# A two-layer mixer behind two attentions: the next batch's work in fewer, longer runs between the channel tiles

## The chip, the cores and the metric

The kernel runs on one core of one Trainium2 chip. The metric is device time in microseconds (us); less is better.

## The reference

For each of 8 batches there are 8 heads, 576 positions and 64 features a head. Two attentions are added, and a token mixer and a channel mixer follow:

```python
q_d = q.reshape(B, H, Sd, 4, D).mean(axis=3)          # k, v likewise; Sd = 144
out_up = np.repeat(sm_attn(q_d, k_d, v_d), 4, axis=2) # softmax attention on the pooled positions
mask = np.abs(pos[:, None] - pos[None, :]) < 4        # a band of 7 positions
out_local = softmax(where(mask, q @ k.T / 8, -1e9)) @ v
x = (out_up + out_local) as (B, 576, 512)
u = x + (relu(x.T @ w_tok1) @ w_tok2).T               # token mixer, 256 hidden
out = u + relu(u @ w_ch1) @ w_ch2                     # channel mixer, 1536 hidden
```

## The kernel before, in words

The four stages of a batch b are these (the names are those of the profile, where buffer numbers are left out).

- *Pooled attention* (`pooled`, L452 to L505, four pairs of heads): scores `sd` on TensorE (PE, L461), their maxima `mxd` and `nmd` on VectorE (L467, L468), exponentials `pd` on ScalarE (L473), transposes `td` (L480), the copy `ptd` on ScalarE (L483), the product with v `ad` (L489), and the division on VectorE (L495 to L497). A DMA then puts the result `od` beside the windows of v.
- *Local attention* (`local`, L508 to L564, five tiles of 128 or 64 positions): scores `sc` (L521), mask, maximum, difference on VectorE (L528 to L533), exponential on ScalarE (L535), sum, reciprocal and product on VectorE (L538 to L540), transposes `pT` (L544), their copy (L548), and `av` (L557), which adds both attentions in one product.
- *Token mixer* (`mix`, L582 to L671): x is split in two parts `xh` (L597, L599) so that three passes give a precise product (`mm3`, L112); `t1` (products named t by xh and W, L114), the hidden layer `hid` (L633, L635), `t2` (L621, L114), the copies `u` (L646) and their maxima `umx` (L648). Then comes the scale of the channel mixer's input, one chain for each chunk of positions (256 and 320): a maximum over the partitions by a transpose `um_t` (L573), a reduction (L576) and a broadcast `um_b` (L579); the scale by three small instructions (`pow2`, L118 to L120); and for each of the four blocks of 128 channels the split `uh` into a high half on ScalarE (L665) and a low half on VectorE (L667).
- *Channel mixer* (`first` and `second`, L722 and L747 onwards): 12 tiles of `c` by CW and uh, each of 12 products (L114), their relu split `h` in two halves (L742 on ScalarE, L744 on VectorE), then four tiles of `c` by CX and h, each of 36 products, and their addition to u (L770) and DMA out. In the text a "c product" is one of these matmuls, on 256 or 320 columns.

PSUM is divided by hand: two double banks "gg" (sd, td, sc, av, t1, t2), three banks "m" (c), one bank "g" (ad, pT, um).

The first 220 us are ordered by a planner with engine clocks (`drive`). What the change touches is the steady loop behind it, for b = 1 to 7 (L863 on). There the channel mixer of batch b is written out, and after each of its pieces `tick` issues some of batch b+1's side work: all the three stages above, and the loads of batch b+2. The side work comes from one generator (`side`, L711; `together` lets three attention pieces take turns). Each step says its engine and its estimated time; only the time of TensorE's steps is counted, and 0.05 for every step. `tick` has a target that grows with the channel mixer's columns done, up to 42 / 0.9, and issues side steps as long as their count stands below it. When a batch begins, `while ("uh", b, ch) not in made: work.go()` issues whatever is still lacking for its uh.

The loop stands outside of `tc.manual_schedule()`. So the order in which steps are issued is a priority, and the framework's scheduler still moves instructions: one that it reckons to be ready may pass one that waits. What came out is read from the built program.

Of the kernel before, what the change touches and what calls it, by code (L numbers as in the profile page):

```python
# [27 lines left out]
FR = 0.9  # L28
# [6 lines left out]
def tile_ups_attention_mixer(ctx, tc, qk, vw, vr, w1, w2, c1, c2, out):  # L35

    nc = tc.nc
    B, _, S = out.shape
# [100 lines left out]
    def may(d):  # L139
        return all(n in made for n in d[2])  # L140
# [570 lines left out]
    def side(b):  # L711

        if b < B:
            st = ready[b]
            yield from attention(st)
            m = mix(st)
            if b + 1 < B:
                m.append(ahead(b + 1))
            yield from together(m, len(m))


    def first(st, ch, places):  # L722
        b, N = st.b, CHUNKS[ch][1]
        hs = st.h[ch] = []
        for f in range(NF):
            e = yield step("P", 12 * N * 0.43e-3, ("C1", f), ("uh", b, ch),
                           *([("mixed", b)] if places[f // 3] != "h" else []), take=f"m>1{ch}")
            uh = st.uh[ch]
            ps = PM(f"c1_{b}_{ch}_{f}")[:, :N]
            for c in range(4):  # L730
                mm3(ps, lambda a: C1.fin[f][:, a, 128 * c:128 * c + 128], lambda a: uh[c][:, a], c == 0, c == 3)
            if f % 3 == 0:
                three = T([128, 3, 2, NMAX], F16, places[f // 3], f"h{b}_{ch}_{f}")
            hs.append((ps, three[:, f % 3, :, :N]))
            make(("c1", b, ch, f), e)

    def first_up(st, ch):
        b = st.b
        for f in range(NF):
            yield step("A", 0.41, ("c1", b, ch, f))  # L740
            ps, ht = st.h[ch][f]
            nc.scalar.activation(ht[:, 0], ps, AF.Relu)  # L742
            e = yield step("V", 0.46, give=f"m>1{ch}")
            nc.vector.scalar_tensor_tensor(ht[:, 1], ps, 0.0, ht[:, 0], ALU.max, ALU.subtract)  # L744
            make(("h", b, ch, f), e)

    def second(st, ch, banks):  # L747
        b, N = st.b, CHUNKS[ch][1]
        for c in range(4):
            for k in range(3):  # L750
                e = yield step("P", 12 * N * 0.43e-3, ("C2", 4 * k + 3), ("h", b, ch, 4 * k + 3),
                               take="" if k else f"m>2{ch}")
                if k == 0:
                    ps = PM(f"c2_{b}_{ch}_{c}")[:, :N]
                    banks.append(ps)
                for f in range(4 * k, 4 * k + 4):
                    mm3(ps, lambda a: C2.fin[f][:, a, 128 * c:128 * c + 128], lambda a: st.h[ch][f][1][:, a],
                        f == 0, f == NF - 1)
            make(("c2", b, ch, c), e)

    def second_up(st, ch, banks):
        b = st.b
        s0, N = CHUNKS[ch]
        io = T([128, 1], F32, "sc", f"io{b}_{ch}")
        for c in range(4):
            e = yield step("V", 0.53, ("c2", b, ch, c), give=f"m>2{ch}")
            us = st.u[ch]
            if c == 0:
                nc.vector.tensor_mul(io, st.ui[ch], ic)
            nc.vector.scalar_tensor_tensor(us[c], banks[c], io, us[c], ALU.mult, ALU.add)  # L770
            nc.sync.dma_start(out[b, 128 * c:128 * c + 128, s0:s0 + N], us[c])
        make(("over", b, ch), e)


    def through(*gs):
        for g in gs:
            yield from g
# [14 lines left out]
    def lazily(what, *needs):  # L792
        yield step("S", 0.0, *needs)
        yield from what()
# [44 lines left out]
    def rest(items):  # L839
        while items:  # L840
            some = False
            for it in list(items):
                if it[1] is None:
                    items.remove(it)
                elif may(it[1]):
                    some = True
                    yield it[1]
                    it[1] = next(it[0], None)
            if items and not some:
                yield items[0][1]  # L850
# [9 lines left out]
            self.next = next(self.g, None)  # L860
            return d[1] * (d[0] == "P") + 0.05

    SIDE = 42.0  # L863
    work = Run(rest(left))
    for b in range(1, B):
        st = ready[b]
        if b + 1 < B:
            work.g = through(work.g, lazily(lambda b=b: side(b + 1), ("q", b + 1, 3)))
            if work.next is None:
                work.next = next(work.g, None)  # L870
        done = [0, 0.0]

        def tick(n):
            done[0] += n
            while work.next is not None and done[1] < SIDE * done[0] / (FR * 24 * S) and may(work.next):
                done[1] += work.go()

        for ch in range(2):
            while ("uh", b, ch) not in made:
                work.go()  # L880
            banks = []
            g, u = Run(first(st, ch, ["h"] * 4)), Run(first_up(st, ch))
            for _ in range(NF):
                g.go()
                u.go()
                u.go()
                tick(CHUNKS[ch][1])
            g, u = Run(second(st, ch, banks)), Run(second_up(st, ch, banks))
            for c in range(4):
                for k in range(3):  # L890
                    g.go()
                    if k == 2:
                        u.go()
                    tick(CHUNKS[ch][1])
# [50 lines left out]
```

## Time and profile before

| | |
|---|---|
| median of 3 runs | 963.68 us (960.68 to 964.9) |
| span of the profiled execution | 963.2 us |
| mean granted TensorE clock | 0.979 |
| PE busy | 920.6 us, 96% |
| VectorE (DVE), ScalarE (ACT), GpSimd (POOL) busy | 46%, 33%, 24% |
| batch 1 begins its channel mixer at | 223.0 us |
| batch 7's channel mixer begins and ends at | 889.1 and 963.2 us |

The profiled execution's own time is its span; the median of the runs lies 0.5 us above it. In the views, a row of a timeline is start, duration, engine, line, operation, out<-in and count, with the engine's idle time before it in brackets; a row of groups ends in busy time, mean ns of one, and the idle time before with what ended it; a row of waits is who waited for whom, us in total, times, longest. PE ends are modelled and include the pipeline's tail, so that neighbours overlap.

### The profile page before, as it was taken

The page shows a single profiled execution, that of the slowest core. Times are in us where ns is not written, and L with a number is a line of the kernel's source. Part 1 is how long each engine was busy: PE and PEld are TensorE (multiplying, and loading weights), DVE is VectorE, ACT ScalarE, POOL GpSimd, SP SyncE. Part 2 cuts the span into 40 slices and gives each one's busy share as a digit, 9 for nine tenths or more (in the row PEclk, how much of TensorE's full clock was granted, in tenths as well). Part 3 has the DMA queues.
Part 4 walks back from the last instruction along what each step waited for, and adds up shares of the span by engine and source line. Part 5 has one row for each costly group of instructions (what it writes and reads, how often), then busy time and mean ns, then how long its engine had stood idle before and what let it go on. Part 6 is the DMA issues. An engine that isn't in the chain of part 4 may idle for free. (4 is left out here: it accounts for less than half of the span.)

```text
span 963.2 us, 25951 instructions
## 1 busy us (share of the span) xinstructions
PE 920.6 (96%) x11426; PEld 710.8 (74%) x11426; DVE 440.5 (46%) x1058; ACT 314.3 (33%) x723; POOL 228.5 (24%) x361
## 2 busy tenths in 40 slices
PE   6887799999999999999999999999999999999998
PEld 3465577877877788677877778777876778777876
DVE  6777787325352354324453253524453254523221
ACT  2464545214242152314232152413423143422110
POOL 5599960420321003400223003400124000000000
PEclk9777999999999999999999999999999999999999
DMA  8773330620250002500232002500034000000000
GB/s 245 235 278 98 119 80 15 176 64 20 75 155 25 21 20 66 163 14 15 63 126 58 21 9 80 166 7 21 27 82 140 15 14 26 14 1 21 19 12 28
DMA packets 28224, 68.31 MB, mean 71 GB/s; under 512 B 3504, under 2 KB 14000, under 8 KB 26864
## 3 DMA queue, kind: packets, MB, share of 16 engines
q1 hardware_dynamic: 25552, 64.30, 22.0%
q10 hardware_dynamic: 2560, 2.36, 0.9%
q8 instruction: 89, 1.46, 0.6%
q14 instruction: 23, 0.19, 0.1%
HBM read 54.85 MB, written 9.44 MB: 67 GB/s over the span
## 5 line engine op out<-in xcount | busy, mean ns | idle before, releaser
L114 PE MATMUL c<-uh,CW 128*128 128x256 f16 (+1 forms) x2304 | 308.5, 286 | 1.6 <-DVE h L744 1.0
L114 PE MATMUL c<-h,CX 128*128 128x256 f16 (+1 forms) x2304 | 306.9, 286 | 0.0
L114 PEld LDWEIGHTS <-CW 128*128 128x128 f16 x2304 | 216.5, 98 | 68.5 <-issue 15.8
L114 PEld LDWEIGHTS <-CX 128*128 128x128 f16 x2304 | 216.5, 98 | 58.3 <-issue 1.4
L744 DVE SCALAR_TENSOR_TENSOR h<-c,h 128x320 f16<-128x320 f32 (+1 forms) x192 | 87.3, 455 | 161.7 <-ACT h L742 161.6
L742 ACT ACTIVATE h<-c 128x320 f16<-128x320 f32 (+1 forms) x192 | 78.4, 409 | 184.6 <-PE c L114 183.9
L409 POOL TENSOR_TENSOR vr<-vr 72x256 f32<-72x256 f32 x64 | 47.4, 741 | 340.2 <-ACT ptd L483 266.5
L770 DVE SCALAR_TENSOR_TENSOR u<-c,io,u 128x256 f32<-128x256 f32 (+1 forms) x64 | 33.0, 515 | 132.2 <-PE c L114 132.1
L646 ACT COPY u<-t 128x256 f32<-128x256 f32 (+1 forms) x64 | 25.4, 399 | 149.4 <-PE t L114 117.4
L435 POOL TENSOR_TENSOR qs<-qk 128x288 f32<-128x288 f32 x56 | 39.9, 712 | 135.2 <-DMA qk<-in_qk_dram 131.4
L114 PE MATMUL t<-xh,W 128*128 128x512 f32 (+1 forms) x240 | 69.6, 425 | 1.6 <-DVE xh L599 1.4
L648 DVE TENSOR_REDUCE umx<-t 128x1 f32<-128x256 f32 (+1 forms) x64 | 29.2, 457 | 84.8 <-ACT u L646 69.6
L114 PE MATMUL t<-W,hid 128*128 128x256 f32 (+1 forms) x384 | 68.0, 313 | 0.0
L114 PEld LDWEIGHTS t<-W,hid 128*128 128x128 f32 x384 | 54.0, 192 | 2.2
L114 PEld LDWEIGHTS t<-xh,W 128*128 128x128 f32 (+1 forms) x240 | 44.6, 196 | 14.0 <-issue 2.4
L562 ACT COPY x<-av 128x512 f32<-128x512 f32 (+1 forms) x40 | 23.1, 577 | 82.8 <-PE av L557 80.9
L473 ACT ACTIVATE pd<-sd,nmd 72x144 f32<-72x144 f32 x128 | 38.9, 376 | 28.5 <-DVE nmd L468 23.1
L489 PE MATMUL ad<-vd,ptd 72*72 72x65 f32 x512 | 39.4, 229 | 5.1 <-issue 4.7
L489 PEld LDWEIGHTS ad<-vd,ptd 72*72 72x72 f32 x512 | 37.4, 146 | 7.0 <-issue 5.4
L557 PE MATMUL av<-vw,pt 47*32 47x64 f32 x2304 | 35.6, 229 | 5.8 <-DMA vw<-od 3.8
L557 PEld LDWEIGHTS av<-vw,pt 47*32 47x32 f32 x2304 | 27.8, 108 | 16.2 <-issue 8.2
L599 DVE TENSOR_TENSOR xh<-x,xh 128x512 fp32r<-128x512 f32 (+1 forms) x40 | 31.2, 784 | 17.0 <-ACT xh L597 16.9
(107 smaller groups left out, 905.0 us busy)
## 6 DMA issues: line engine op xcount, KB each, us to landing
qk<-in_qk_dram SPq DMA_DIRECT2D x32, 579.0 KB
vw<-in_vw_dram SPq DMA_DIRECT2D x32, 351.0 KB
vr<-in_vr_dram SPq DMA_DIRECT2D x64, 144.0 KB
C_raw<-in_c_dram SPq DMA_DIRECT2D x16, 512.0 KB
out_dram<-u SPq DMA_DIRECT2D x32, 160.0 KB
C_raws<-in_c_dram SPq DMA_DIRECT2D x8, 512.0 KB
out_dram<-u SPq DMA_DIRECT2D x32, 128.0 KB
vw<-od ACTq DMA_DIRECT2D x32, 72.0 KB
```

Source lines behind the costliest of these rows:

```text
L114: nc.tensor.matmul(ps, lhs(a), rhs(c), start=first and i == 0, stop=last and i == 2, **kw)
L409: nc.gpsimd.tensor_add(t[:, 0:2], t[:, 0:2], t[:, 2:4])
L435: nc.gpsimd.tensor_add(two, x[:, :, 0:2], x[:, :, 2:4])
L473: nc.scalar.activation(pd[:, par, g], s[:, par, g], AF.Exp, bias=nm[:, par, g:g + 1], scale=0.125 / 16)
L489: nc.tensor.matmul(ps[:, g, par], pt[:, par, kg, G * g:G * g + G], st.vd[:, kg, 2 * pr + par], start=kg == 0, stop=kg == 1)
L557: nc.tensor.matmul(ps[QB * j:QB * j + QB, par, D * hp:D * hp + D], pt[p, hp, QB * j:QB * j + QB], st.vw[h][p, g, D * hp:D * hp + D], start ...
L599: nc.vector.tensor_tensor(xh[:, 1], xf(t), xh[:, 0].bitcast(F32), ALU.subtract)
L646: nc.scalar.copy(u, ps)
L648: nc.vector.tensor_reduce(umx[ch][:, c:c + 1], ps, axis=AX.X, op=ALU.max, apply_absolute_value=True)
L742: nc.scalar.activation(ht[:, 0], ps, AF.Relu)
L744: nc.vector.scalar_tensor_tensor(ht[:, 1], ps, 0.0, ht[:, 0], ALU.max, ALU.subtract)
L770: nc.vector.scalar_tensor_tensor(us[c], banks[c], io, us[c], ALU.mult, ALU.add)
```

## The change

`tick` gets a second condition. It returns at once unless the side work's count is at least CLUMP = 3.0 us behind the target; then it issues steps until it has caught up, as before. SIDE and FR stay as they are.

```diff
-    SIDE = 42.0
+    SIDE, CLUMP = 42.0, 3.0
...
         def tick(n):
             done[0] += n
+            if done[1] + CLUMP > SIDE * done[0] / (FR * 24 * S):
+                return
             while work.next is not None and done[1] < SIDE * done[0] / (FR * 24 * S) and may(work.next):
                 done[1] += work.go()
```

Three places of the built program show what moves; the names carry batch, chunk and piece (`um5_0_t` is batch 5, chunk 0; `sd6_0` the first pair of heads of batch 6; `c2_4_1_3` the last tile of batch 4's second layer).

First TensorE between the last c tile of batch 4 and the first of batch 5. Before, um_t stands ahead of the last tile:

```order
L114 MATMUL c2_4_1_2_8939<-h4_1_9_8727,CX5_1141 128x320
L573 MATMUL um5_0_t_9007<-ident_61,um5_0_m_9002 1x128
L114 LDWEIGHTS CX0_1136
L114 MATMUL c2_4_1_3_9010<-h4_1_0_8425,CX0_1136 128x320
L114 LDWEIGHTS CX0_1136
```

Now it follows the last product of that tile:

```order
L114 MATMUL c2_4_1_3_8967<-h4_1_9_8727,CX5_1141 128x320
L573 MATMUL um5_0_t_9046<-ident_61,um5_0_m_9015 1x128
L461 MATMUL sd6_0_9165<-qd6_8646 72x144 x4
L579 MATMUL um5_0_b_9053<-um5_0_m1_9048,ones_66 128x1
L461 MATMUL sd6_1_9172<-qd6_8646 72x144 x4
L573 MATMUL um5_1_t_9142<-ident_61,um5_1_m_9140 1x128
L480 MATMUL td6_0_9193<-ident_61,pd6_0_9183 72x72
L579 MATMUL um5_1_b_9146<-um5_1_m1_9144,ones_66 128x1
L480 MATMUL td6_0_9193<-ident_61,pd6_0_9183 72x72 x5
L114 LDWEIGHTS CW0_134
L114 MATMUL c1_5_0_0_9078<-uh5_0_0_9063,CW0_134 128x256
```

The whole chain of the scale, for both chunks, stands between two c products, with batch 6's first sd and td among it. The same holds at the boundaries of batches 2 to 6; at the last one there is no sd and td.

Second VectorE at the same place. Before, the scale's instructions follow each other:

```order
L576 TENSOR_REDUCE um5_0_m1_9009<-um5_0_t_9007 1x1
L570 TENSOR_REDUCE um5_1_m_9064<-umx5_1_9001 128x1
L118 TENSOR_SCALAR ui5_0_9029<-um5_0_b_9027 128x1
L119 TENSOR_SCALAR ui5_0_9029<-ui5_0_9029 128x1
L120 RECIPROCAL us5_0_9030<-ui5_0_9029 128x1
L667 SCALAR_TENSOR_TENSOR uh5_0_0_9037<-u5_0_0_8821,us5_0_9030,uh5_0_0_9037 128x256
```

Now the maxima of sd stand among them:

```order
L770 SCALAR_TENSOR_TENSOR u4_1_3_7559<-c2_4_1_3_8967,io4_1_8760,u4_1_3_7559 128x320
L576 TENSOR_REDUCE um5_0_m1_9048<-um5_0_t_9046 1x1
L570 TENSOR_REDUCE um5_1_m_9140<-umx5_1_9014 128x1
L467 TENSOR_REDUCE mxd6_0_9170<-sd6_0_9165 72x4
L118 TENSOR_SCALAR ui5_0_9055<-um5_0_b_9053 128x1
L468 TENSOR_SCALAR nmd6_0_9171<-mxd6_0_9170 72x4
L119 TENSOR_SCALAR ui5_0_9055<-ui5_0_9055 128x1
L467 TENSOR_REDUCE mxd6_1_9177<-sd6_1_9172 72x4
L120 RECIPROCAL us5_0_9056<-ui5_0_9055 128x1
L576 TENSOR_REDUCE um5_1_m1_9144<-um5_1_t_9142 1x1
```

So the reciprocal L120 stands behind both maxima, and the reduction for the second um_b behind L120.

Third TensorE at the local attention's last tile. Before, 24 c products and av_3 stand between sc_4 and pT_4 (two whole tiles of 12, one ahead of av_3 and one behind it); this is the end of the second tile:

```order
L114 MATMUL c1_4_1_1_8463<-uh4_1_3_7594,CW1_135 128x320
L544 MATMUL pT5_4_8489<-ident_61,P2_110 128x64 x4
L114 LDWEIGHTS CW2_136
L114 MATMUL c1_4_1_2_8513<-uh4_1_0_7585,CW2_136 128x320
L114 LDWEIGHTS CW2_136
```

Now av_3 comes at once behind sc_4, then five c products, a stretch of t1 and one more c product; this is the end of the five and what follows them:

```order
L114 MATMUL c1_4_1_4_8570<-uh4_1_1_7650,CW4_138 128x320
L114 MATMUL t1_5_8563<-xh5_0_8546,W1_0_148 128x512 x6
L114 LDWEIGHTS CW4_138
L114 MATMUL c1_4_1_4_8570<-uh4_1_1_7650,CW4_138 128x320
L544 MATMUL pT5_4_8520<-ident_61,P2_110 128x64 x4
```

Six c products stand in the gap where 24 stood, and a t1 stretch has come in.

## The prediction

> **What bounds the kernel now.** I read the page first, then the busy times batch by batch, then the chain that ended last, then the waits, then the timeline at the places that the change moves. "Boundary" is the place on TensorE between the last product of one batch's second channel layer and the first of the next batch's first layer.
>
> ```profile
> span 963.2 us, 25951 instructions
> ```
>
> The busy times of each engine in the steady batches 1 to 6 (length, then PE's busy time):
>
> ```profile
> 223.01:332.87 109.86, 108.74 (x1398) 85.38 (x1397) 46.38 (x120) 35.41 (x84) 19.79 (x38) 1.00 0.20 59
> 332.87:445.90 113.03, 110.67 (x1407) 86.07 (x1406) 48.77 (x123) 36.00 (x85) 19.32 (x37) 1.00 0.20 59
> 445.90:557.12 111.22, 108.94 (x1406) 85.51 (x1406) 46.47 (x121) 34.64 (x83) 19.41 (x37) 1.00 0.20 60
> 557.12:667.95 110.83, 108.92 (x1407) 85.50 (x1404) 46.31 (x117) 34.55 (x83) 19.38 (x37) 1.00 0.20 60
> 667.95:779.06 111.11, 108.91 (x1406) 85.54 (x1404) 46.22 (x117) 34.58 (x83) 19.52 (x37) 1.00 0.21 60
> 779.06:889.14 110.08, 108.78 (x1406) 85.51 (x1404) 46.11 (x119) 35.33 (x84) 0.00 (x0) 1.00 0.05 15
> ```
>
> TensorE sets the time: it idles 1.12 + 2.36 + 2.28 + 1.91 + 2.20 + 1.30 = 11.2 us in the 666 us of these six batches, and no other engine is busy for half of them. The change adds and removes no arithmetic, so it can win what is left of this idle time and the price of turning from one kind of product to another, and it can lose by putting waits where there were none. The chain shows the turns:
>
> ```profile
> 790.33 1.03 PE ad L489 x16
> 791.36 1.31 PE c L114 x12
> 792.68 0.64 PE sd L461 x8
> 793.32 1.42 PE c L114 x12
> ...
> 798.92 0.50 PE td L480 x8
> 799.42 1.31 PE c L114 x12
> ...
> 836.93 1.39 PE t L114 x6
> ```
>
> Twelve c products take 1.31 us after ad or td and 1.42 us after sd: most turns are free, and one out of sd costs 0.11 us.
>
> **The runs.** In the built order a steady batch had 43 stretches of side work between c products and now has 31. Of the 12 that vanish the td, ad and t ones cost nothing to begin with; about three (sd, sc, av) carry 0.1 to 0.2 us each, the larger end doubling the measured 0.11 for an entry as well as an exit. I take 0.4 us a batch: 6 x 0.4 = **-2.4 us**, between 0 and -4.
>
> **The boundary.** The debt rule leaves up to 3 us of side work unissued when a batch ends, and its tail is the scale of the next batch: um_t, um_b, the scale, the splits uh. They were issued among the last c products; now they stand at the boundary, where c can't go on before uh is there. Before, the same chain ran under c products, at the last boundary so:
>
> ```profile
> 883.20 0.27 PE L573 MATMUL um_t<-ident,um_m 128*1 128x128 f32 x1
> ...
> 883.41 0.55 DVE L770 SCALAR_TENSOR_TENSOR u<-c,io,u 128x320 f32<-128x320 f32 x1 [1.35 <-PE c L114]
> 883.87 0.27 DVE L576 TENSOR_REDUCE um_m<-um_t 1x1 f32<-1x128 f32 x1
> ...
> 884.22 0.38 PE L579 MATMUL um_b<-um_m,ones 1*128 1x1 f32 x2
> ...
> 884.64 0.16 DVE L118 TENSOR_SCALAR ui<-um_b 128x1 uint32<-128x1 uint32 x1 [0.43 <-PE um_b L579]
> ...
> 885.27 1.70 ACT L665 ACTIVATE uh<-u,us 128x256 f16<-128x256 f32 x4 [3.74 <-DVE us L120]
> ...
> 885.82 0.48 DVE L667 SCALAR_TENSOR_TENSOR uh<-u,us,uh 128x256 f16<-128x256 f32 x1 [0.64 <-ACT uh L665]
> ```
> ```profile
> L467 DVE TENSOR_REDUCE mxd<-sd 72x4 f32<-72x576 f32 x32 | 23.6, 746 | 5.1 <-PE sd L461 5.1
> PE td L480 <- ACT pd L473: 4.8, 7, 1.0
> PEld um_b L579 <- issue: 1.4, 6, 0.3
> ```
>
> Counted from um_t, um_b starts at 1.02 us, the scale is ready at 2.0, the first uh low half at 3.1; the other three follow at 0.42 each (1.70 for four on ScalarE), so the last is there at 4.4. At the last boundary nothing else is left to do: the first c tile needs all four and ends near 4.9 us; TensorE's own work in that is um_t and um_b twice (about 1.0 us, since um_t's end overlaps what follows) and 15 c products of 0.109 (1.6 us): 2.3 us idle. At the other five the next batch's sd and td are pulled in as fillers, but their maxima (L467) stand on VectorE ahead of the scale: the first from 1.0 to 1.75; L118, L468, L119 to 2.25; the second waits for sd_1, which stands behind um_b, and runs 2.3 to 3.05; the scale is ready at 3.2; the second um_b, which waits for its reduction behind that scale, goes at 3.55; the rest of td_0 ends at 4.25, and only then may c start. The low halves come at 4.8, 5.4, 5.8, 6.2, and the first c tile ends at 6.4. Work in these 6.4 us: um 1.0, two sd 1.3, td 0.5, 15 c 1.6, together 4.4: 2.0 us idle. Sum: 5 x 2.0 + 2.3 = 12.3. What goes is the wait of td for the exponentials at the same place (4.8 in seven) and the issue of um_b (1.4 in six): 6.2. Net **+6.1 us**; bounds: if the fillers cover the chain but for 0.5 us a boundary, 3 - 6.2 = -3; if each chain runs bare at 4 us, +18.
>
> A granted clock that falls would add to this. Where little ran, the trace has it (stretches of the clock's own step, PE busy second, clock third from the end):
>
> ```profile
> 57.02:60.43 3.41, 2.02 (x101) 1.60 (x79) 2.06 (x5) 2.36 (x5) 3.17 (x4) 1.00 0.90 310
> 60.43:63.84 3.41, 3.41 (x53) 2.51 (x39) 2.10 (x7) 2.56 (x5) 3.25 (x3) 0.50 0.97 352
> ...
> 91.15:94.56 3.41, 2.15 (x15) 1.48 (x15) 1.78 (x4) 0.70 (x2) 3.25 (x3) 1.00 0.63 196
> 94.56:97.98 3.42, 3.01 (x22) 2.25 (x21) 2.41 (x7) 1.46 (x3) 3.18 (x4) 1.00 0.30 119
> ```
>
> After 2.02 us busy of 3.41 the clock was 0.50 in the next stretch, after 2.15 it stayed 1.00. At the five boundaries I count some 2.2 to 2.4 us busy in the worst 3.41, so I put no clock into the sum; it is a rival. The Trainium skill (TensorE: Matmul & The Clock Gate, HAM oscillation) asks only that no idle gap exceed about 3.4 us; by that rule no boundary could lose clock and the sum would stay. The rows above disagree with it: the stretch that lost its clock was busy for 2.02 us.
>
> **Inside the batch.** Tile 4's softmax stood under two c tiles and stands under less now. Before, from sc to its transpose:
>
> ```profile
> 608.00 0.48 PE L521 MATMUL sc<-qk 64*32 64x38 f32 x32
> ...
> 608.42 1.80 PE L114 MATMUL c<-uh,CW 128*128 128x320 f16 x12
> ...
> 609.47 0.46 DVE L528 TENSOR_TENSOR P<-sc,mask 64x304 f32<-64x304 f32 x1
> ...
> 610.15 0.86 PE L557 MATMUL av<-vw,pt 47*32 47x64 f32 x64
> ...
> 612.18 0.47 DVE L540 TENSOR_TENSOR P<-P,r 64x304 f32<-64x304 f32 x1
> ...
> 612.71 0.46 PE L544 MATMUL pT<-ident,P 64*128 64x64 f32 x4
> ```
> ```profile
> L744 DVE SCALAR_TENSOR_TENSOR h<-c,h 128x320 f16<-128x320 f32 (+1 forms) x192 | 87.3, 455 | 161.7 <-ACT h L742 161.6
> L742 ACT ACTIVATE h<-c 128x320 f16<-128x320 f32 (+1 forms) x192 | 78.4, 409 | 184.6 <-PE c L114 183.9
> L497 DVE TENSOR_TENSOR od<-ad,rd 72x256 f32<-72x256 f32 x32 | 13.5, 421 | 1.1
> L496 DVE RECIPROCAL rd<-rd 72x4 f32<-72x4 f32 x32 | 5.6, 174 | 1.1
> L495 DVE TENSOR_SCALAR rd<-ad 72x4 f32<-72x4 f32 x32 | 5.0, 157 | 26.2 <-PE ad L489 26.1
> PEld pT L544 <- PE av L557: 2.3, 4, 0.6
> ```
>
> L528 to L540 takes 3.2 us (609.47 to 612.65). Now TensorE has between sc_4 and pT_4 only sc 0.4 (608.00 to 608.42), av 0.86, six c 0.9 (half of the 1.80), t 1.39: 3.5 us. L528 stands behind the h of the c tile just ended, L742 and L744 with their hops about 1.2 us; so pT_4 is ready at 4.5 and TensorE waits 1.0, of which 0.2 was there before: 6 x 0.8 = **+4.8 us** (0 if that h comes late and is passed over, +7). Two ad stretches now stand with only one sd between; they share one PSUM bank, which comes free after L495, L496, L497 (0.75 us, 1.0 with an h ahead and the hops) against 0.64 to 0.74 of sd: 0.3. ad_2 waits for the copy of td_2 on ScalarE, 576 elements where the 256 of L665 take 0.42, estimated at 0.7 and two hops, against 0.72 of TensorE's work (td_3 and two c): 0.2; ad_3 behind pT likewise 0.1. Sum 6 x 0.6 = **+3.6 us** (0 to +6). The last t1 stretch leaves the hid split 0.15 short: **+0.9** (0 to +2). pT_2's wait (2.3 in four, the last row) mostly goes, since more c stands before it: **-1.5** (-2.3 to 0).
>
> **The sum.** -2.4 + 6.1 + 4.8 + 3.6 + 0.9 - 1.5 = +11.5 us on the profiled 963.2, 974.7. The runs before have a median of 963.68, 0.5 above that span: **975.2 us**. The three large terms may each be off by half; the halves add up to 7, so this case alone reaches from 968 to 982. About 0.5% (4.8 us) is what a measurement of this kernel can tell from no change: under 958.9 is faster, over 968.5 slower.
>
> **The rivals.** *No net change:* the scheduler knows of these chains and has laid fillers in them; if the boundary costs what td's wait cost (6.2) and only tile 4 and the ad bank are left at a third of my price, the sum is -2.4 + 0 + 2.8 + 0.9 - 1.5 = -0.2, so 964. For it speaks that TensorE's idle before is only 11 us although the same kind of packing stood there; against it the second L467 on VectorE, which is fixed by the order. 0.20. *Faster:* the chain at the boundary is hidden to 0.5 us a place (-3.2), no wait arises inside, run prices at their larger end (-4) and pT_2's wait gone (-2): 954. It needs sd's maxima to be read so early that the scale isn't pushed back, that is sd_1 done by 1.75 us after um_t; the order puts it behind um_b. 0.12. *Slower by the clock:* the forecast's waits, and at each of six boundaries a stretch with at most 2.02 us busy, so that the next 3.41 us run at half: 1.7 us x 6 = +10, 985. It decides from some 0.2 us more idle at a boundary than I count, or a stretch that falls badly. 0.16. That the order doesn't change is excluded by the built program.
>
> **How the numbers follow.** Forecast 0.52, of which 0.02 would come out within 0.5%; no change 0.20; faster 0.12; clock 0.16. So faster 0.12, same 0.22, slower 0.66. The range takes in the forecast, no change and the nearer half of the clock's case (to 986) and leaves out most of the faster one: 958 to 986.
>
> **What would show it.** Right: at six boundaries um_t follows the last c product directly, c's first tile waits about 2 us in all for uh, and pT_4 waits about 1 us for L540; PE's idle time per batch rises from 1.9 to near 4 us, with PE's busy time unchanged within 0.5 us. Wrong: idle at the boundary at or under 1 us; pT_4 without a wait; a clock of 0.50 after 110 us; or a busy time per batch that falls by more than 0.7 us, which would say that turns cost more than I priced.

## The result and the profile after

The changed kernel takes 994.2 us (990.5 to 995.7) against 962.2 for the kernel before on the same chip: a ratio of 1.032, with a 95% interval from 1.029 to 1.035. It is slower, as forecast, but the forecast was 975.2 and its range ended at 986. The profiled execution has a span of 994.0 us, 30.8 over the 963.2 of before.

First the busy times of each engine in batches 1 to 6 of the changed kernel (start and end, length, PE's busy time; the granted clock stands third from the end):

```profile
226.27:342.47 116.20, 112.71 (x1421) 87.36 (x1421) 48.06 (x127) 36.17 (x89) 19.08 (x37) 1.00 0.20 57
342.47:456.70 114.23, 110.56 (x1408) 86.39 (x1406) 45.26 (x118) 34.49 (x83) 19.08 (x37) 1.00 0.21 58
456.70:573.08 116.38, 112.02 (x1408) 87.21 (x1405) 46.51 (x118) 34.48 (x83) 19.03 (x37) 0.99 0.19 57
573.08:688.96 115.88, 112.01 (x1407) 87.22 (x1405) 45.54 (x118) 34.47 (x83) 19.34 (x37) 0.99 0.20 57
688.96:804.56 115.60, 112.01 (x1408) 87.25 (x1406) 45.91 (x118) 34.48 (x83) 19.18 (x37) 0.99 0.20 58
804.56:918.07 113.51, 110.21 (x1385) 85.77 (x1383) 43.90 (x112) 32.95 (x78) 0.00 (x0) 0.98 0.05 15
sum 691.80, PE 669.51 PEld 521.20 DVE 275.18 ACT 207.04 POOL 95.71; mean PE 111.59 PEld 86.87 DVE 45.86 ACT 34.51 POOL 15.95
```

The 30.8 us split so. Batch 1 begins 3.3 us later (226.27 for 223.01), though up to there the order of the instructions is the same. In the other kernels' profiles the same moment lies anywhere from 218.8 to 226.3, so I take these 3.3 for chance. Batches 1 to 6 take 691.8 us for 666.1: +25.7. The last batch takes 1.8 more. In the six batches PE idles 691.8 - 669.5 = 22.3 us, where it idled 11.2, and its busy time has grown by 14.5 as well, which the prediction had expected to stay.

Nearly half of the growth in busy time is the clock. These are stretches of the clock's own step at four boundaries of the changed kernel, each with the stretch behind it:

```profile
338.13:341.54 3.41, 2.32 (x23) 1.37 (x21) 2.85 (x11) 1.14 (x5) 0.00 (x0) 1.00 0.14 48
341.54:344.96 3.42, 3.32 (x30) 2.78 (x31) 2.69 (x10) 3.34 (x9) 0.00 (x0) 1.00 0.00 0
454.18:457.59 3.41, 2.30 (x25) 1.70 (x21) 2.50 (x14) 2.96 (x9) 0.00 (x0) 1.00 0.13 45
457.59:461.01 3.42, 3.42 (x19) 2.42 (x17) 3.17 (x9) 2.34 (x6) 0.00 (x0) 0.50 0.00 0
...
686.28:689.70 3.42, 2.31 (x24) 1.74 (x23) 2.52 (x13) 2.81 (x9) 0.00 (x0) 1.00 0.14 48
689.70:693.11 3.41, 3.41 (x18) 2.45 (x17) 3.01 (x9) 2.38 (x6) 0.00 (x0) 0.50 0.00 0
...
914.97:918.38 3.41, 2.07 (x14) 1.32 (x13) 1.76 (x9) 0.86 (x3) 0.00 (x0) 1.00 0.14 48
918.38:921.80 3.42, 3.27 (x17) 2.20 (x16) 2.31 (x9) 1.48 (x5) 0.00 (x0) 0.50 0.00 0
```

Five of the six boundaries are followed by 3.41 us at clock 0.50; the kernel before has no such stretch after 110 us. Each costs about 1.7 us: four within the six batches, 6.8, and the fifth nearly all of the last batch's 1.8.

The waits of TensorE in batches 1 to 6, in the kernel before:

```profile
PE td L480 <- ACT pd L473: 4.5, 6, 1.0
PE av L557 <- DMA vw<-od: 1.7, 3, 0.8
PE pT L544 <- DVE P L540: 1.3, 4, 0.3
...
PE sc L521 <- ACT pd L473: 0.9, 2, 0.4
```

and in the changed one:

```profile
PE pT L544 <- DVE P L540: 6.6, 18, 0.6
PE td L480 <- ACT pd L473: 5.8, 6, 1.1
PE av L557 <- DMA vw<-od: 3.2, 4, 1.3
PE ad L489 <- DVE od L497: 2.2, 6, 0.4
PE sc L521 <- ACT pd L473: 2.1, 6, 0.3
```

The rows of pT, ad, td and sc grew, by 10 us together, pT's alone by 5.3, and the growth is spread: three pT per batch, one ad, one sc. The row of av for its DMA grew by 1.5, but two other waits of av, 1.9 in all, went, so that av as a whole waits no longer than before (3.2 for 3.7). The first part of each wait does not even show, as this piece of TensorE's timeline in batch 4 tells (the idle time stands in the bracket):

```profile
587.25 1.20 PE L489 MATMUL ad<-vd,ptd 72*72 72x65 f32 x16
588.38 0.71 PE L461 MATMUL sd<-qd 64*72 64x144 f32 x8
589.46 1.22 PE L489 MATMUL ad<-vd,ptd 72*72 72x65 f32 x16 [0.36 <-DVE od L497]
590.61 0.71 PE L461 MATMUL sd<-qd 64*72 64x144 f32 x8
591.26 1.48 PE L114 MATMUL c<-uh,CW 128*128 128x256 f16 x12
593.09 0.78 PE L521 MATMUL sc<-qk 64*32 64x38 f32 x64 [0.35 <-ACT pd L473]
```

Here ad_1 waits for the bank that ad_0 used, and sc_0 for a bank that the exponentials of sd_2 and sd_3 still read. Twelve c products at 0.109 are 1.31 us, but the row says 1.48: the modelled end of the last one covers 0.17 of the wait that follows. So sc_0 waits 0.52, not 0.35. The 7.7 us of busy time that the clock does not explain (14.5 - 6.8) would be 45 such beginnings, seven or eight per batch. That number is worked out, not counted. The time itself can be had from the starts alone. When each product is given the median distance from its start to the next start (of like products at full clock, over seven of the profiles), the six batches need 618.7 us before and 618.8 after. What goes beyond is idle time that the rows show (11.2, then 22.3), half clock (none, then 6.7) and delays under modelled ends (36.2, then 44.1, so 7.9 more).

### The profile page after: what moved, and what is told of

Same layout as the page of the kernel before. It is cut to its first block, busy times and chain, and to the rows that moved or that the text cites. A ratio compares the mean times of both kernels' runs of the same rounds, so it can differ in the third digit from the quotient of the medians.

```text
span 994.0 us, 25915 instructions
## 1 busy us (share of the span) xinstructions
PE 936.0 (94%) x11417; PEld 719.8 (72%) x11426; DVE 438.0 (44%) x1058; ACT 312.7 (31%) x723; POOL 226.2 (23%) x361
## 4 chain that ended last, share of the span: by engine, by line
PE 64%; DVE 7%; DMA 2%; ACT 2%; issue 1%; ACTq 0%; POOL 0%
PE c L114 46%; PE t L114 8%; PE ad L489 3%; DMA vw<-od 2%; PE t L621 2%; PE av L557 1%; PE pT L544 1%; ACT pd L473 1%; PE td L480 1%; PE sc L521 1%; DVE P L533 1%; DVE P L540 1%; DVE r L538 1%; DVE mx L532 1%; DVE u L770 1%
## 5 line engine op out<-in xcount | busy, mean ns | idle before, releaser
L114 PE MATMUL c<-h,CX 128*128 128x256 f16 (+1 forms) x2304 | 303.3, 286 | 0.0
L114 PEld LDWEIGHTS <-CW 128*128 128x128 f16 x2304 | 223.6, 99 | 66.6 <-issue 7.5
L114 PEld LDWEIGHTS <-CX 128*128 128x128 f16 x2304 | 218.8, 98 | 57.7 <-issue 1.4
L770 DVE SCALAR_TENSOR_TENSOR u<-c,io,u 128x256 f32<-128x256 f32 (+1 forms) x64 | 33.1, 517 | 162.6 <-PE c L114 162.4
L114 PE MATMUL t<-W,hid 128*128 128x256 f32 (+1 forms) x384 | 73.2, 320 | 0.0
L114 PE MATMUL t<-xh,W 128*128 128x512 f32 (+1 forms) x240 | 64.8, 413 | 1.6 <-DVE xh L599 1.4
L114 PEld LDWEIGHTS t<-xh,W 128*128 128x128 f32 (+1 forms) x240 | 44.1, 191 | 14.9 <-issue 1.8
L548 ACT COPY pt<-pT 128x512 f32<-128x512 f32 (+1 forms) x40 | 21.6, 542 | 39.5 <-PE pT L544 39.2
```

Source lines behind the costliest of these rows:

```text
L114: nc.tensor.matmul(ps, lhs(a), rhs(c), start=first and i == 0, stop=last and i == 2, **kw)
```

## The experiments

Fifteen kernels were run. They share one question: which part of the change costs what, and do the parts add? In the edits, `done[0]` is the count of columns of the channel mixer, 24 S in a batch: the first chunk ends at 10.7 S, token mixing begins near 12.9 S, the second chunk's first layer ends at 17.4 S, its last c tile begins at 22.3 S. Ratios are to the kernel before, with 95% intervals.

**The end spread again.**

```diff
-            if done[1] + CLUMP > SIDE * done[0] / (FR * 24 * S):
+            if done[0] <= 17.4 * S and done[1] + CLUMP > SIDE * done[0] / (FR * 24 * S):
```

> The work is issued in long runs only up to the middle of a batch's second chunk; from there on, and so at the end of a batch with the um chain, it is spread as before. Theory A (most of the loss is waits inside the batches, +3 to +3.5 us in each of six, where a product is met too early by what feeds it; the rest, some +8.5 us, is half clock at five batch boundaries): the half-clock stretches after 110 us go, the waits of ad, sc and pT stay, 978 to 983 us. Theory B (the end of the batch with its clock is the whole loss, the longer runs inside cost nothing): 962 to 966 us.

Measured: 974.2 us, 1.0103 (1.0069 to 1.0137), and no half clock after 110 us. It lies between the two theories, nearer to A: long runs inside do cost, but by this run 10 us of the 31, not 20.

**The end alone.**

```diff
-            if done[1] + CLUMP > SIDE * done[0] / (FR * 24 * S):
+            if done[0] > 22.3 * S and done[1] + CLUMP > SIDE * done[0] / (FR * 24 * S):
```

> The other part alone: inside a batch the work is spread as before, and only the last piece (from the first layer of the last c tile on: sd, td and the um chain) is held back to the boundary as in the changed kernel. Theory A: one half-clock stretch of 3.41 us at each of about five boundaries, 1.7 us each, and 0 to 0.5 us of waiting at each, so 969 to 975 us. Theory B: the whole loss, 985 to 994 us.

Measured: 971.2 us, 1.0068 (1.0047 to 1.0088), as theory A has it, but for the number of half-clock stretches. Three boundaries lose clock in the same way, not five; these are one that did (from batch 3 to 4) and one that did not (from 1 to 2):

```profile
554.12:557.53 3.41, 2.28 (x22) 1.54 (x22) 2.78 (x11) 1.65 (x6) 0.00 (x0) 1.00 0.14 48
557.53:560.95 3.42, 3.42 (x21) 2.75 (x21) 3.19 (x11) 3.02 (x7) 0.00 (x0) 0.50 0.01 2
...
332.26:335.67 3.41, 2.07 (x16) 1.56 (x17) 3.32 (x12) 2.63 (x9) 0.00 (x0) 1.00 0.00 0
335.67:339.09 3.42, 3.42 (x33) 2.76 (x32) 2.75 (x9) 2.70 (x7) 0.00 (x0) 1.00 0.00 0
```

Three times 1.7 is 5.1 of the 6.7 us; about 1.6 is left for all waiting at the boundaries. The split is rough: the 6.7 is that of the median, and the profiled execution is the shortest of the ten (967.8 us).

**Six products of no use at each boundary.**

```diff
         for ch in range(2):
             while ("uh", b, ch) not in made:
                 work.go()
+            if ch == 0:
+                ps = PM("busy")
+                for _ in range(6):
+                    nc.tensor.matmul(ps, junk[:, :128], junk, start=True, stop=True)
```

> The changed kernel with six products of 128x512 more at each batch boundary, whose result nobody reads; they fill TensorE while the um chain runs on the other engines. If the half clock at the boundaries comes from too little busy time in a stretch of 3.41 us, these stretches come out at full clock (at most one of five left), and the time falls by 4 to 8 us below the changed kernel, to 986 to 990 us, although the kernel does more. If the clock there does not hang on TensorE's own busy time, the half-clock stretches stay and the time is 994 to 1003 us.

Measured: 989.1 us, 1.0248 (1.0200 to 1.0297). The boundary from batch 4 to 5 (686.28 in the changed kernel's rows), with the clock's step where this run had it, and one more place:

```profile
679.99:683.40 3.41, 3.36 (x22) 1.79 (x21) 1.55 (x7) 0.52 (x2) 0.00 (x0) 1.00 0.14 48
683.40:686.82 3.42, 3.42 (x31) 2.92 (x32) 2.80 (x11) 2.49 (x7) 0.00 (x0) 1.00 0.02 5
720.95:724.36 3.41, 1.75 (x74) 1.22 (x72) 1.43 (x3) 0.00 (x0) 2.58 (x5) 1.00 0.56 157
724.36:727.78 3.42, 3.42 (x78) 2.33 (x77) 0.48 (x1) 0.00 (x0) 1.68 (x4) 0.50 0.04 13
```

All the half-clock stretches at boundaries are gone, so the clock there hangs on TensorE's own busy time. The modelled amount alone does not decide: 2.07 us kept the full clock in the kernel with the end alone and lost it at the changed kernel's last boundary. The one half-clock stretch that is left followed a wait of av for its DMA, far from a boundary. What the products are worth as a repair is not settled. The median is 5.1 us below the changed kernel's, as expected. But from batch 1 on the profiled execution, the longest of its four, is no shorter than the changed kernel's (990.0 - 221.8 = 768.2 us against 994.0 - 226.3 = 767.7): six products take 1.3 us to win back 1.7, and the stretch that is left costs 1.7.

**A smaller and a larger threshold.**

```diff
-    SIDE, CLUMP = 42.0, 3.0
+    SIDE, CLUMP = 42.0, 1.0
```

and 6.0 in the other kernel.

> The changed kernel with the threshold at 1.0 in place of 3.0: shorter runs, and the um chain stays in the last c tile. Theory A: no half clock after 110 us, the waits inside the batches about a third of those of the changed kernel (+1 us per batch), 966 to 972 us. Theory B (only the boundary costs): 962 to 965 us.

> The changed kernel with the threshold doubled, 6.0 in place of 3.0: about half as many runs, twice as long, and a boundary that holds um, sd and more of td. Theory A (waits inside the batches grow with what stands in one run, and the boundary holds more work whose feeders are late): 1003 to 1020 us, at least one half-clock stretch at each boundary. Rival (the loss is the boundary's half clock alone, one stretch whatever the length): 992 to 998 us.

Measured: 972.9 us, 1.0081 (1.0050 to 1.0112) with 1.0, just above what theory A gives and far from B, with one half-clock stretch that A had excluded (behind waits of av, inside a batch); and 986.7 us, 1.0230 (1.0198 to 1.0262) with 6.0. Both theories fail on the second: twice the length costs less than the change itself, and only three boundaries lose clock. The loss does not grow with the length of the runs alone; what stands where is the next question.

**Parts of a batch.** Long runs in the first chunk only, and (second line) in the token mixing only:

```diff
-            if done[1] + CLUMP > SIDE * done[0] / (FR * 24 * S):
+            if done[0] <= 10.7 * S and done[1] + CLUMP > SIDE * done[0] / (FR * 24 * S):
+            if 12.9 * S < done[0] <= 22.3 * S and done[1] + CLUMP > SIDE * done[0] / (FR * 24 * S):
```

> Longer runs only while a batch's first chunk is worked on (first 10.7 of the batch's 24 S columns); after that the work is spread as before. It splits the run with the spread end, which was 9.9 us slower than the kernel before, its steady batches 111.9 us against 111.0. If the cost sits where attention's first products stand in runs (ad, sc_0, pT_0: some 0.5 to 1.3 us per batch of waits for pd and for od): 967 to 973 us. If it sits in the second chunk (pT_4 behind P, runs of t products, 0.8 to 1.0 per batch): 962 to 966 us.

> Longer runs only where the side work is the token mixing of the next batch (from 12.9 to 22.3 of the batch's 24 S columns): there a run holds 12 to 18 products of one kind, and the profile shows hardly a wait; attention and the um chain stay as before. Theory A (the longer runs cost where they hold a chain of attention, and at the boundary): no loss, and the turns saved, 3 or 4 per batch, give at most 0.4 us each batch, 960 to 965 us. Rival (a long run costs by its length, for instance because the banks of the c and t products come free later): 0.8 to 1.1 us more per batch, as the t and t2 runs of the changed kernel took together against those of the kernel before, 968 to 972 us.

Measured: 973.2 us, 1.0085 (1.0054 to 1.0117) for the first chunk, at the upper end of its first case; 965.4 us, 1.0010 (0.9982 to 1.0039) for token mixing, as theory A has it. So the first chunk's attention carries the whole cost of the run with its end spread. Alone, long runs of t products cost nothing that can be told, and they win nothing either.

**Two kernels without long runs, all side work earlier.** Each is the kernel before with one number changed:

```diff
-    SIDE = 42.0
+    SIDE = 46.0
```

```diff
-        done = [0, 0.0]
+        done = [0, -2.5]
```

> The kernel before with the rate of its side work raised from 42 to 46 per batch, so that each step comes up to 9% of a batch earlier and the um chain ends some four products of c before the boundary; no run is made longer on purpose. If only long runs cost: 962 to 965 us. If every step's place against the engines that feed it matters (theory A in its general form): the waits of pT for P and of av for vw change by a microsecond per batch one way or the other, 957 to 972 us, and the um chain's waits at the boundary fall to nothing.

> The kernel before with the count of its side work begun at -2.5 in each batch: every step comes about three products of c earlier, no run is made longer by a rule, and no clump is at the boundary. If a step's place against what feeds it on the other engines is what costs (theory A): waits of td for pd, of av for vw and of pT for P grow by 1 to 2.5 us per batch, 970 to 980 us. If long runs cost by themselves: 962 to 967 us.

Measured: 975.5 us, 1.0104 (1.0064 to 1.0143) with the higher rate, 962.7 us, 0.9999 (0.9975 to 1.0024) with the early count. The first lies outside of both its cases, the second is where it should be if only long runs cost. Together they contradict a simple rule: the first shows that 11 us can be lost with no long run at all, the second that coming early is not by itself what costs. Why the higher rate is slower stays open; two stretches of half clock are in its profile, and c products that waited 4.9 us for nothing that it shows.

**Do the parts add?** Without the long runs from 17.4 S to 22.3 S (the later part of token mixing), and with the first chunk and the end only:

```diff
-            if done[1] + CLUMP > SIDE * done[0] / (FR * 24 * S):
+            if not 17.4 * S < done[0] <= 22.3 * S and done[1] + CLUMP > SIDE * done[0] / (FR * 24 * S):
+            if not 10.7 * S < done[0] <= 22.3 * S and done[1] + CLUMP > SIDE * done[0] / (FR * 24 * S):
```

> The changed kernel without its long runs of the token mixing (from 17.4 to 22.3 of a batch's 24 S columns the work is spread again); attention's long runs and the boundary stay. The runs of token mixing alone cost 1.2 us over the kernel before, less than such a comparison tells. If they cost nothing here either, and what is left carries the loss: 989 to 996 us. If the loss needs them too, as the spread end (974 us) and the end alone (971 us) add to 981 us only: 978 to 985 us.

> Long runs in a batch's first chunk and at its end (sd, td and the um chain at the boundary); the second chunk is spread. The first chunk alone cost 9.1 us over the kernel before, the end alone 6.7. If the two add: 977 to 983 us. If the boundary shifts the first chunk's runs, so that pT_1, pT_2 and av_0 come at places where what feeds them is late (2.4 us more per batch in the changed kernel than in the one with its end spread): 985 to 993 us.

Measured: 980.6 us, 1.0174 (1.0124 to 1.0225) and 980.4 us, 1.0188 (1.0137 to 1.0239). The first chunk's +9.1 and the end's +6.7 make 15.8, near to the +17.2 that the two give together. But then some 14 us are missing up to the changed kernel, and they come with token mixing's long runs, which had cost 1.2 by themselves; the first of the two kernels says that it takes those behind 17.4 S. The clock is the smaller part of the 14: three half-clock stretches after 110 us in the second kernel, five in the changed one, so 3.4 us. Two more kernels ask where: the end and token mixing without the first chunk, and all but the second chunk's attention.

```diff
-            if done[1] + CLUMP > SIDE * done[0] / (FR * 24 * S):
+            if done[0] > 12.9 * S and done[1] + CLUMP > SIDE * done[0] / (FR * 24 * S):
+            if not 10.7 * S < done[0] <= 12.9 * S and done[1] + CLUMP > SIDE * done[0] / (FR * 24 * S):
```

> Long runs only from 12.9 of a batch's 24 S columns on: token mixing and the end with its boundary; attention in both chunks is spread. Theory C (token mixing's long runs cost nothing by themselves; they move the steps of the next batch's attention so that, in long runs, pT, av and ad come where what feeds them is late): the end's 6.7 us and 1 more, 968 to 975 us. Rival (token mixing's runs and the boundary cost together, by half clock or a late um chain): 979 to 988 us.

> The whole change but for attention's part in the second chunk (from 10.7 to 12.9 of a batch's 24 S columns the work is spread). In the order of the instructions the first chunk's runs stand as in the changed kernel: ad_0, sd_2, ad_1 and sd_3 in one run, pT_1 behind the first chunk's end. Theory C: 987 to 995 us, as the changed kernel. Rival (the loss sits in the second chunk's long runs of pT and av): 977 to 984 us.

Measured: 971.1 us, 1.0072 (1.0046 to 1.0099) and 992.7 us, 1.0285 (1.0250 to 1.0320), both as theory C has them. Token mixing's long runs cost where the first chunk's long runs are there too, and not without. The longest wait of TensorE in batches 1 to 6 without the first chunk's long runs (sc's follows with 2.6 us, and the view has no row of av, pT or ad):

```profile
PE td L480 <- ACT pd L473: 5.8, 6, 1.1
```

and with them:

```profile
PE td L480 <- ACT pd L473: 5.8, 6, 1.1
PE av L557 <- DMA vw<-od: 3.4, 5, 1.0
PE pT L544 <- DVE P L540: 3.4, 12, 0.4
PE ad L489 <- DVE od L497: 2.2, 6, 0.4
...
PE av L557 <- ACT x L562: 1.8, 6, 0.3
```

The boundary does not make the difference: td waits 5.8 in both, and both have five half-clock stretches after 110 us. The six batches take 674.6 us without those runs and 692.0 with them. Of these 17.4 us 10.0 are idle time, nearly all of it at av, pT and ad; the other 7.4 are busy time, and that these are the covered beginnings of the same waits is argued, not shown. The order of TensorE's instructions says what token mixing's runs move. In the kernel with the first chunk and the end only, the first chunk's long runs are ad_0, some c products, and then ad_1, sd_2, sd_3; with token mixing's runs it is ad_0, sd_2, ad_1, sd_3 in one run, the piece of timeline shown above. And pT_1 comes after the first chunk's last c tile instead of before its end. In the changed kernel, batch 4:

```profile
620.26 0.48 DVE L770 SCALAR_TENSOR_TENSOR u<-c,io,u 128x256 f32<-128x256 f32 x1 [3.45 <-PE c L114]
...
621.93 0.47 DVE L540 TENSOR_TENSOR P<-P,r 128x304 f32<-128x304 f32 x1
...
622.45 0.65 PE L544 MATMUL pT<-ident,P 128*128 128x128 f32 x4 [0.20 <-DVE P L540]
```

P_1's last steps (L538 to L540) stand on VectorE behind L770, which waits for that c tile; from L770's start they need 2.1 us, and pT_1 comes before they are done.

**A version meant to beat both.** First the first td one product later in the kernel before:

```diff
-        yield step("P", 0.6, ("q", b, pr), *([("pair", b, pr - 2)] if pr > 1 else []), take="gg")
+        yield step("P", 0.6 + 0.5 * (b > 1 and pr == 1), ("q", b, pr), *([("pair", b, pr - 2)] if pr > 1 else []), take="gg")
...
-        yield step("P", 0.5, take="gg", give="w")
+        yield step("P", 0.5 - 0.5 * (b > 1 and pr == 1), take="gg", give="w")
```

Then the same with 3.0 in place of the added and subtracted 0.5, and the early count besides.

> The kernel before with the first td of each batch one product of c later (a cost in the planner's list is moved from td to sd); nothing else moves. The first td waits 0.7 to 1.0 us per batch for pd in the kernel before. If that wait goes and nothing takes its place: 3 to 5 us faster, 959 to 962 us. If the wait moves on to ad behind it (both stand closer now): no change, 963 to 966 us.

> The kernel before with the count of its side work begun at -2.5 in each batch, and with the first td held back by one product of c (a cost moved from sd to td in the planner's list): a version meant to be faster than both. The first td waits 0.7 us in each steady batch with the early count alone. If that wait goes and ad behind it waits 0.2 to 0.3: 959 to 962 us; if ad takes over the whole wait: 962 to 966 us.

Measured: 963.2 us, 0.9986 (0.9964 to 1.0009), no difference that can be told; then 961.5 us, 0.9974 (0.9956 to 0.9992), faster than the kernel before by a quarter of a percent, and so than both. It is a small gain, and what the later td adds to the early count (0.9999) is not told apart from nothing. In the first, td's wait went from 4.8 to 3.8 us only. With the early count alone td waits so:

```profile
PE td L480 <- ACT pd L473: 3.8, 6, 0.7
```

and in the last kernel so, with new waits of ad and sc:

```profile
PE ad L489 <- DVE od L497: 2.2, 6, 0.4
...
PE sc L521 <- ACT pd L473: 1.7, 5, 0.3
...
PE td L480 <- ACT pd L473: 0.2, 1, 0.2
```

3.6 us went, and 2.2 at ad and 1.7 at sc came: the wait moved on and did not go. TensorE's idle time in batches 1 to 6 is 8.3 us with the early count alone and 8.8 in the last kernel.

## Why the prediction was wrong

The sign was right, and most places were named. The sum was +11.5 where +30.8 came, 3.3 of which I take for chance. Three steps failed: the clock, put at nothing; the boundary's waiting, counted too high before a credit that never came; and the waits inside the batch, looked for in three places only.

**The clock** was the largest miss at one step. "After 2.02 us busy of 3.41 the clock was 0.50 in the next stretch, after 2.15 it stayed 1.00": from these two rows I took a threshold and put no clock into the sum. At the boundaries 2.30 and 2.31 lost the clock, 2.32 kept it once. The busy time that the profile models does not by itself tell which way the clock goes (2.07 later went both ways), and one pair of rows could not exclude a loss. The count of 2.2 to 2.4 us in the worst stretch was right. The rival had the mechanism and the price (1.7 us each); its condition, at most 2.02 us busy, was wrong. It cost 8.5 us at five boundaries. The Trainium skill (TensorE: Matmul & The Clock Gate, HAM oscillation) asks that no idle gap exceed about 3.4 us. By that rule no boundary could lose clock; it does not hold here, since the longest idle gap at the boundary quoted next is 1.11 us, a third of it.

**The boundary's waiting**, +6.1, was mis-sized, though its chain came out as worked up to the first low half. In the changed kernel, from batch 4 to batch 5:

```profile
684.80 0.27 PE L573 MATMUL um_t<-ident,um_m 128*1 128x128 f32 x1
...
688.12 0.26 PE L480 MATMUL td<-ident,pd 72*72 72x72 f32 x1 [1.11 <-ACT pd L473]
...
688.96 0.49 PE L114 MATMUL c<-uh,CW 128*128 128x256 f16 x3
688.99 0.47 DVE L667 SCALAR_TENSOR_TENSOR uh<-u,us,uh 128x256 f16<-128x256 f32 x1
```

c starts 4.16 us after um_t, where I had 4.25, and the first low half is there at 4.66, where I had 4.8. But the forecast had c's first tile wait about 2 us for uh, and the whole profile has 0.3 us of such waiting, as before. The half clock did not hide it. At the boundary from batch 1 to 2, which kept the full clock, c starts 4.16 us after um_t as well and then runs on, 20 products in 2.50 us, no more than 0.15 over their 0.109 each and the last one's tail:

```profile
342.47 0.49 PE L114 MATMUL c<-uh,CW 128*128 128x256 f16 x3
...
343.03 2.50 PE L114 MATMUL c<-uh,CW 128*128 128x256 f16 x20
```

So TensorE idles 1.2 us (1.11 of it on td's row) at each of the five boundaries where I had 2.0, and 1.3 at the last where I had 2.3: 7.3 for 12.3. The 6.2 that I took off again did not go. td's wait (4.5 in the six batches) grew to 5.8, nearly all of it now at the boundary, and the 1.4 of um_b came from a row of PEld, the weight loads, which overlap PE; PE itself had idled only 0.2 us ahead of um_b. Net, the boundaries idle some 2.8 us more. Alone, the end cost 6.7 us, and some 5 of that are clock: that this is near the 6.1 of the sum is luck.

**Inside the batch** the forecast priced three places (tile 4, the ad bank, hid) and took pT_2's wait away: +7.8. What the chance, the clock (8.5) and the boundaries (2.8) leave of the 30.8 is some 16 us, about half idle time in the rows above and half covered. Three faults:

- "TensorE waits 1.0" for pT_4, at a net 0.8. It idles 0.51 on this row of batch 4, and with the part that is covered 0.7:

```profile
635.92 0.46 PE L544 MATMUL pT<-ident,P 64*128 64x64 f32 x4 [0.51 <-DVE P L540]
```

  A wait of this kind is not the main loss: with the second chunk's attention spread, twelve c products stand before pT_4, and the time is still 992.7.
- ad_1 at the bank, priced 0.3, waits 0.36 on its row and 0.5 with the covered part. "pT_2's wait mostly goes" was wrong: two rows of pT per batch besides pT_4's are among the 18, and the 2.3 it was taken from is again a row of PEld.
- The places that I did not look at cost most. sc_0 waits for the exponentials of sd_2 and sd_3, which now come just before it; pT_1 stands behind the first chunk's end. I had costed three places and taken the rest as free; each long run in attention should have been followed to what feeds the step behind it.

**The runs**, -2.4: nothing of it shows. Long runs of token mixing alone, where no wait can hide a gain, gave +1.2 us (-1.7 to +3.8).

Of the signs that were named beforehand, PE's idle time per batch came out as said (from 1.9 to 3.3 to 4.4 us), and um_t follows the last c product. PE's busy time, which was to stay within 0.5 us, grew by 2.4 a batch, and a clock of 0.50 after 110 us, which was to count as wrong, is there. The rivals without a loss fell with the sign. hid's +0.9 can't be read from a row.

The range missed because the halves of its three terms allowed for a wrong size at a named place and not for places left out, and because the clock's case was taken in only up to 986.

## What to carry to other kernels

Between the products of one stage, a chain through several engines needs distance, and the distance of each step is set by what is issued with it: two parts of a reordering measured alone may add up to little more than half of what they cost together, so the whole has to be run. Where TensorE has to wait anyway, look at the clock's steps and not only at the wait: a stretch of 3.41 us with about 2.3 us of modelled busy time can cost 1.7 us in the next one, more than the wait itself. Before longer runs are tried to save turns, one part in which nothing waits should show that a turn costs anything.

## What the runs showed of the hardware

The clock's steps lie on a fixed raster of 3.41 us, and a batch can lock to it. With token mixing and end in long runs, two half-clock stretches in succession are

```profile
332.55:335.96 3.41, 3.41 (x19) 2.56 (x18) 3.01 (x9) 2.06 (x6) 0.00 (x0) 0.50 0.00 0
...
445.19:448.60 3.41, 3.41 (x20) 2.48 (x18) 2.87 (x10) 2.22 (x6) 0.00 (x0) 0.50 0.00 0
```

112.64 us apart, 33 steps of 3.4133, while its batches 2 to 5 take 112.5 to 112.6 us. In the changed kernel two of the quoted stretches, two batches apart, are 689.70 - 457.59 = 232.11 us apart, 68 steps. So each boundary meets the raster at nearly the same place, and five lose clock in each of these two kernels, three in the one with the end alone. After 110 us no stretch at full clock with 2.33 us or more of modelled busy time was followed by half clock in any of the seventeen profiles; between 1.99 and 2.31 us it went both ways. A stretch at half clock is another case: once, in the kernel without long runs from 17.4 S to 22.3 S, one that was busy throughout (3.41 us, from 569.7) was followed by a second. Whether the half clock itself draws the batch to a whole number of steps was not tried.
